# Fused attention and MLP backward: attention blocks in two passes, with a key quarter's exponentials turned by DMA

## The chip, the cores and the metric

The kernel runs on one core of a Trainium2 chip. The core has five engines with instruction streams of their own: PE (TensorE, matmuls), DVE (VectorE), ACT (ScalarE), POOL (GpSimd) and SP (SyncE, which here only issues DMAs). They run unsynchronized and wait for each other at semaphores. The metric is device time in microseconds of one execution, here the median of three runs: 2291.8 us (2291.62 to 2293.79). The profile is of one further execution.

## The reference

The program computes a forward pass and all gradients of it. With `xn = layernorm(x)`:

```python
def _A_ref(x, wqkv, wo):            # B, S, D = 1, 2048, 512; H = 32 heads, Dh = 16
    q, k, v = split_heads(x @ wqkv)
    scores = einsum("bhqd,bhkd->bhqk", q, k) * (Dh ** -0.5)
    p = softmax(scores)
    return merge_heads(einsum("bhqk,bhkd->bhqd", p, v)) @ wo

def _B_ref(x, w1, b1, w2, b2):      # F = 1792
    h = gelu(layernorm(x) @ w1 + b1)
    return h @ w2 + b2

out = x + _A_ref(xn, wqkv, wo) * silu(_B_ref(xn, w1, b1, w2, b2))
```

Outputs are `out` and the gradients of x, wqkv, wo, w1, b1, w2 and b2 for a given `grad_out`. In the backward pass of attention, with dO the gradient of a head's output, the gradient of the scores is dS = P * (dO V^T - rowsum(dO * O)). From it come dQ = dS K / 4 and dK = dS^T Q, and dV = P^T dO.

## The kernel before

There are three stages. `phase_pre` does the layernorms, projections and the MLP forward; attention starts near 157 us of the profile and ends near 1945; `phase3` does the remaining gradients. The change is in attention, with small parts of the other two.

`attention_core` handles the 32 heads in 16 pairs (p), the 2048 queries in four quarters (qc): 64 blocks (j). A block has 16 steps, one for each 128 keys (kb); a step index g counts through all blocks. All tiles hold two heads side by side, so a step's score tile is 128 keys x 2 x 512 queries.

In a step, `emit_s` (L1064) makes the scores with keys on the partitions, and ACT's exponential (L1092) writes them to `et`. Softmax sums aren't known yet, so `et` is not normalized; a shift taken off in the operands keeps it in range. `emit_d` (L1086) makes dO V^T for each head in a PSUM bank of its own, and DVE multiplies it with `et` into `gts` (L1103, two per step). `emit_a1` adds up over the steps, in the PSUM tile X, V and K weighted with `et` (L1126) and, through the constant `Lc`, the sums (L1123); `emit_a2` (L1136) adds the same for `gts`. After 16 steps X is copied out (L1141), transposed on PE in f32 (L1148), copied again (L1153), and `emit_finish` computes 1/sum, the row sums and, on POOL, the weights W1, W2, the outputs `Oall` and dQ in `dQall`.

For dK and dV the same matrices are needed with queries on the partitions. Each two steps' `gts` (128 x 2048 bf16) is turned by one DMA transpose issued by SP (L1112), into half of a map `gk` that holds one key quarter (kc). The exponentials are made a second time with queries on the partitions: `emit_t` (L1076) and ACT (L1097) into `e`. For one step in four of three key quarters they are turned instead, by eight PE transposes (L1048) and a DVE copy (L1053, `eE`). `emit_ze` (L1196) and `emit_zg` (L1204) add into the 64-row PSUM tile Z, with W1 and W2 as weights, and DVE adds Z into `acc` (L1219, L1221) or, in the last query quarter, into `ob` (L1223), which SP stores (L1225). This runs one block behind.

Once a pair, `load_pair` reads three operand tables (L1006 to L1008), POOL pads them into `KPad` and `QPad`, and SP turns these into KVT and QDT (L1019, L1022).

PE and DVE follow orders written out by hand for one block (`PE_ORDER`, `DVE_ORDER`), which a loop unrolls; ACT alternates the two kinds of exponentials. SP and POOL instructions are issued where the loop meets them. The MLP's last four token tiles and the last dO projections (`left_over`) are spread over the first 14 steps.

What matters of buffers: `et` 8 tiles of a step, `gts` 4 tiles of two steps, `gk` 6 maps, score tiles in PSUM 2, `d` one bank a head, and one bank shared in turn by Z, XT and ET.

Of the kernel before, what the change touches and what calls it, by code (L numbers as in the profile page):

```python
# [41 lines left out]
def phase_pre(ctx, tc, k, A_x, A_wqkv, A_wo, B_w1, B_b1, B_w2, B_b2, grad_out, opnds, psz, tailp):  # L42
# [138 lines left out]
    def kv_tile(g, i):  # L181
        proj(g, i, D, "pk", NS[g][:, :, i, :, 1:17])
        proj(g, i, 2 * D, "pv", NS[g][:, :, i, :, 17:33])
        proj(g, i, 0, "pq", NQ[:, :, 4 * g + i, :, 1:17])
        if i == 3:
            ts = slice(4 * g, 4 * g + 4)
            ns = NS[g]
            nc.sync.dma_start(out=k.NAT_s[g], in_=ns[:].rearrange("p a t j c -> p a t (j c)"))
            nc.gpsimd.tensor_copy(out=KPad[:, ts, 0:2, 0:17], in_=ns[:, 0, :, :, 0:17])
            nc.gpsimd.tensor_copy(out=KPad[:, ts, 2:4, 0:16], in_=ns[:, 0, :, :, 17:33])  # L190
            nc.gpsimd.tensor_copy(out=OP0["NAT"][:, ts], in_=ns[:, 0])
# [12 lines left out]
    def k_norm(g, i):  # L204
        norms(p1, kn2[:, 4 * g + i, :], NS[g][:, :, i, :, 1:17])

    with tc.manual_schedule(engines={ET_.PE, ET_.Activation, ET_.DVE, ET_.Pool, ET_.SP}):
# [4 lines left out]
        for g in range(4):  # L212
            NS[g] = p1.tile([128, NPAIR, 4, 2, NATW], bf16, name="NS", bufs=4)
            nc.gpsimd.memset(NS[g][:, :, :, :, 0:1], 1.0)
# [142 lines left out]
    def do_done(g):  # L357
        ts = slice(4 * g, 4 * g + 4)
        nd0 = ND[g][:, 0].rearrange("p t (j c) -> p t j c", j=2)
        nc.gpsimd.tensor_copy(out=QPad[:, ts, 2:4, 0:16], in_=nd0)  # L360
        if g >= 1:
            turn_q(g)
        nc.sync.dma_start(out=k.NATQd_s[g], in_=ND[g])
        nc.gpsimd.tensor_copy(out=OP0["NATQd"][:, ts], in_=nd0)

    def left_over(big, mid2, xt2, st2):


        w = [big.tile([128, 2, 16, 128], bf16, name="gk")[:].rearrange("p a b c -> p (a b c)") for _ in range(3)]

# [8 lines left out]
        load_do(3)  # L379
        v = {}  # L380

        def z(nm):
            return psz.tile([128, 512], f32, name=nm, tag="z")

        def first(t):
            m_mm(t, z("ps_m15"), 0, 7)

        def second(t):
            m_mm(t, None, 7, FC)
# [4 lines left out]
            th = xt2.tile([128, 4, 128], f32, name="xt")  # L394
            m_sig(mq[:, 0, :], th[:].rearrange("p a b -> p (a b)"), s[:, 0, :])
# [6 lines left out]
        def rest2(t):  # L402
            m_grad2(t, *v[t][0:3])

        def turn(_):
            pt = st2.tile([128, 4, IC, 128], bf16, name="dso_tp", tag="st")
            for i in range(4):
                for b in range(IC):
                    nc.tensor.transpose(pt[:, i, b, :], dso4[3][:, i, b * 128:(b + 1) * 128], k.ident_bf[:])
            nc.scalar.copy(out=dsoT[3], in_=pt[:])  # L410

        def do(t):

            g, i = divmod(t, 4)
            pd = st2.tile([128, 2, 512], f32, name="pd", tag="st")
# [3 lines left out]
            nc.scalar.copy(out=ND[g][:, :, i:i + 2, :].rearrange("p a n c -> p n a c"), in_=pd[:].rearrange("p n (a c) -> p n a c", a=NPAIR))  # L419
            if i == 2:  # L420
                do_done(g)
        steps = {g: [[], []] for g in range(14)}
        for n, t in enumerate(range(12, 16)):
            steps[2 * n][1].append((first, t))
            steps[2 * n + 1][1].append((second, t))
            steps[2 * n + 2][0].append((rest1, t))
            steps[2 * n + 3][0].append((rest2, t))
        for g, f in ((8, (do, 8)), (9, (do, 10)), (10, (turn, 0)), (11, (do, 12)), (12, (do, 14))):
            steps[g][1].append(f)
        def fill(_):  # L430
            w = z("fill")
            for n in range(2):
                nc.tensor.matmul(w[:], lhsT=woT[:, 0, 0:128], rhs=woT[:, 0, :], start=(n == 0), stop=(n == 1))
        steps[13][0].append((fill, 0))
        steps[13][1].append((fill, 0))
        return steps

# [16 lines left out]
    def row_shift3():  # L454
        for ts in (slice(0, 4), slice(4, 16)):
# [3 lines left out]
            if ts.start == 0:  # L459
                turn_q(0)  # L460
# [74 lines left out]
def phase3(ctx, tc, k, A_x, A_wqkv, A_wo, B_w1, B_w2, grad_out, out_0, out_1, out_2, out_3, out_4, out_5, out_6, out_7, dbg):  # L535
# [14 lines left out]
    with ExitStack() as c1:  # L550
# [13 lines left out]
        with ExitStack() as cL:  # L564
# [289 lines left out]
            dQT = dT.tile([128, NT, IC, 128], bf16, name="dQT", tag="dT")  # L854

            def turn_dq(q4):
                nc.sync.dma_start_transpose(out=dQT[:, q4 * 4:(q4 + 1) * 4].rearrange("p t c s -> p (t c) s"),
                                            in_=k.dQall[:, q4 * 4:(q4 + 1) * 4, :].rearrange("p t d -> p (t d)"))

            def load_r(h):  # L860
                nc.sync.dma_start(out=R[:, 4 * h:4 * h + 4], in_=k.dKVT_s.rearrange("(r p) s -> p r s", p=128)[:, 4 * h:4 * h + 4])
            later = [lambda: turn_dq(0), lambda: nc.sync.dma_start_transpose(out=wqT[:], in_=A_wqkv[:, 0:D]),
                     lambda: nc.sync.dma_start_transpose(out=wkvT[:], in_=k.WKVA_s), lambda: load_r(0), lambda: load_r(1),
                     lambda: turn_dq(1), lambda: turn_dq(2), lambda: turn_dq(3)]
# [15 lines left out]
        with ExitStack() as c2:  # L880
# [33 lines left out]
            for t in range(NT):  # L914
# [6 lines left out]
                for cc in range(IC):  # L921
                    nc.tensor.matmul(ps[:], lhsT=dQT[:, t, cc, :], rhs=wqT[:, cc, :], start=(cc == 0), stop=False)
# [27 lines left out]
PE_ORDER = """  # L950
a2:-1 zg:-7 d1:1 t:1 ze:-6 s:2 d0:1 zg:-6 ze:-5 zg:-5 t:2 d1:2 a1:0 s:3 d0:2 XT:-1 d1:3 s:4 a1:1 a1:2 t:4 d0:3 a2:0 ze:-4
a2:1 zg:-4 a2:2 ze:-3 s:5 d1:4 zg:-3 ze:-2 t:5 d0:4 zg:-2 ze:-1 zg:-1 s:6 d1:5 a1:3 a1:4 d0:5 t:6 E:3 s:7 a1:5 d0:6 s:8
d1:6 ze:0 a2:3 zg:0 ze:1 a2:4 t:8 d1:7 zg:1 s:9 d0:7 d1:8 ze:2 a2:5 d0:8 t:9 zg:2 s:10 d1:9 ze:3 a1:6 zg:3 t:10 d0:9 a1:7
a1:8 s:11 d1:10 E:7 s:12 d0:10 a1:9 d1:11 t:12 a1:10 a2:6 ze:4 a2:7 s:13 d0:11 zg:4 d1:12 a2:8 ze:5 d0:12 t:13 zg:5 a2:9
ze:6 a2:10 d1:13 s:14 d0:13 zg:6 a1:11 d1:14 t:14 a2:11 ze:7 zg:7 s:15 d0:14 a1:12 a2:12 d1:15 t:15 E:11 s:16 d0:15 a1:13
d1:16 t:16 a1:14 a2:13 ze:8 a2:14 zg:8 s:17 d0:16 a1:15 ze:9
"""
DVE_ORDER = """
m0:-5 m1:-4 m0:-4 m1:-3 m0:-3 m1:-2 acc:-9 m0:-2 m1:-1 eE:-5 m0:-1 m1:0 m0:0 xs:-1 m1:1 m0:1 acc:-5 m1:2 m0:2 xt:-1 m1:3
m0:3 sm:-1 m1:4 m0:4 acc:-1 m1:5 m0:5 eE:3 m1:6 m0:6 m1:7 m0:7 m1:8 m0:8 m1:9 acc:3 m0:9 m1:10 eE:7 m0:10 m1:11  # L960
"""


# [11 lines left out]
def attention_core(ctx, tc, opnds, ps_z, tail, NAT_s, NATQ_s, Oall, dQall, dKVT_out, ident_f32, ident_bf, npairs=16, nqc=4, turned=(0, 1, 2)):  # L975

    nc = tc.nc  # L980
    S = 2048
    ps_st = ctx.enter_context(tc.tile_pool(name="ps_st", reuse_waits="tile", bufs=2, space=PSUM))
    ps_d = ctx.enter_context(tc.tile_pool(name="ps_d", reuse_waits="tile", bufs=1, space=PSUM))
    ps_x = ctx.enter_context(tc.tile_pool(name="ps_x", reuse_waits="tile", bufs=1, space=PSUM))
    etp = ctx.enter_context(tc.tile_pool(name="etp", reuse_waits="tile", bufs=8))
    gtp = ctx.enter_context(tc.tile_pool(name="gtp", reuse_waits="tile", bufs=4))
    gbp = ctx.enter_context(tc.tile_pool(name="gbp", reuse_waits="tile", bufs=6))
    ep = ctx.enter_context(tc.tile_pool(name="ep", reuse_waits="tile", bufs=8))
    eep = ctx.enter_context(tc.tile_pool(name="eep", reuse_waits="tile", bufs=4))
    xsp = ctx.enter_context(tc.tile_pool(name="xsp", reuse_waits="tile", bufs=1))  # L990
    finp = ctx.enter_context(tc.tile_pool(name="finp", reuse_waits="tile", bufs=2))
    wp = ctx.enter_context(tc.tile_pool(name="wp", reuse_waits="tile", bufs=2))
    accp = ctx.enter_context(tc.tile_pool(name="accp", reuse_waits="tile", bufs=1))
    outp = ctx.enter_context(tc.tile_pool(name="outp", reuse_waits="tile", bufs=1))

    OP = opnds["OP"]
    KPad, QPad, Lc = opnds["KPad"], opnds["QPad"], opnds["Lc"]
    cur_op = {}
    load_q = []

    def load_pair(p):
        t = OP[p % 2]
        cur_op[p] = t

        def plain():
            nc.sync.dma_start(out=t["NAT"][:].rearrange("q (g k) j c -> q g (k j c)", g=4), in_=NAT_s[:, :, p].rearrange("g q k c -> q g (k c)"))  # L1006
            nc.sync.dma_start(out=t["NATQq"][:].rearrange("q k j c -> q (k j c)"), in_=NATQ_s[0][:, p])
            nc.sync.dma_start(out=t["NATQd"][:].rearrange("q (g k) j c -> q g (k j c)", g=4), in_=NATQ_s[1][:, :, p].rearrange("g q k c -> q g (k c)"))  # L1008

        def padk():  # L1010
            nc.gpsimd.tensor_copy(out=KPad[:, :, 0:2, 0:17], in_=t["NAT"][:, :, :, 0:17])
            nc.gpsimd.tensor_copy(out=KPad[:, :, 2:4, 0:16], in_=t["NAT"][:, :, :, 17:33])

        def padq():
            nc.gpsimd.tensor_copy(out=QPad[:, :, 0:2, 0:17], in_=t["NATQq"][:])
            nc.gpsimd.tensor_copy(out=QPad[:, :, 2:4, 0:16], in_=t["NATQd"][:])

        def turnk():
# [438 lines left out]
```

## Time and profile before

| | us |
|---|---|
| median of three runs | 2291.8 |
| the profiled execution, span | 2294.9 |
| attention, first to last transpose L1112 (start) | 169.0 to 1926.5 |
| transposes L1112 | 512, 4.5 from issue to landing (median) |
| PE busy | 2217.2 (97%) |
| DVE busy | 2041.7 (89%) |
| ACT busy | 2030.4 (88%) |
| POOL busy | 358.5 (16%) |
| granted TensorE clock, mean | 0.993 |

An engine's busy time is the time in which at least one of its instructions ran; instructions of one engine can overlap, so a busy engine may still have room, and the distance between two starts says more than a duration. In the profile L12 is line 12 of the kernel, PEld is the load of weights into PE, and "<-" ahead of a name means what ended a wait. SP's rows are the time in which it issued a DMA, not the time of the transfer. In the tables of stretches each engine has its busy time and a count, followed by the granted clock, the share of time that DMA packets were in flight, and GB/s.

### The profile page before, as it was taken

The page shows a single profiled execution, that of the slowest core. Times are in us where ns is not written, and L with a number is a line of the kernel's source. Part 1 is how long each engine was busy: PE and PEld are TensorE (multiplying, and loading weights), DVE is VectorE, ACT ScalarE, POOL GpSimd, SP SyncE. Part 2 cuts the span into 40 slices and gives each one's busy share as a digit, 9 for nine tenths or more (in the row PEclk, how much of TensorE's full clock was granted, in tenths as well). Part 3 has the DMA queues.
Part 4 walks back from the last instruction along what each step waited for, and adds up shares of the span by engine and source line. Part 5 has one row for each costly group of instructions (what it writes and reads, how often), then busy time and mean ns, then how long its engine had stood idle before and what let it go on. Part 6 is the DMA issues. An engine that isn't in the chain of part 4 may idle for free.

```text
span 2294.9 us, 50938 instructions
## 1 busy us (share of the span) xinstructions
PE 2217.2 (97%) x20089; PEld 794.7 (35%) x20135; DVE 2041.7 (89%) x3612; ACT 2030.4 (88%) x2322; POOL 358.5 (16%) x835
## 2 busy tenths in 40 slices
PE   7988999999999999999999999999999999879999
PEld 3433333333333333333333333333333333434544
DVE  7767999999999999999999999999999997789455
ACT  6767999999999999999999999999999998676243
POOL 4321111111111111111111111111111111421000
PEclk9999999999999999999999999999999999989999
DMA  9889999999999999999999999999999898987982
GB/s 290 276 268 181 167 179 164 185 162 183 162 183 164 179 163 180 166 179 170 175 175 166 180 165 184 160 183 165 181 165 179 157 162 208 226 187 151 126 241 70
DMA packets 1309744, 413.46 MB, mean 180 GB/s; under 512 B 1272416, under 2 KB 1286368, under 8 KB 1308864
## 3 DMA queue, kind: packets, MB, share of 16 engines
q1 hardware_dynamic: 1299056, 384.91, 90.5%
q0 software_dynamic: 6528, 20.06, 2.9%
q10 hardware_dynamic: 3920, 5.24, 0.7%
q8 instruction: 157, 2.57, 0.4%
q14 instruction: 83, 0.68, 0.1%
HBM read 44.42 MB, written 49.03 MB: 41 GB/s over the span
## 4 chain that ended last, share of the span: by engine, by line
PE 83%; DVE 8%; issue 4%; DMA 2%; ACT 2%; POOL 1%; SPq 0%; DVEq 0%; ACTq 0%; POOLq 0%
PE d L1086 12%; PE X L1123 12%; PE s L1064 11%; PE Z L1204 9%; PE X L1136 7%; PE Z L1196 5%; DVE gts L1103 5%; PE t L1076 5%; PE ET L1048 5%; PE ps_dw L789 2%; PE ps_dy L872 2%; PE ps_dhg L805 2%; PE XT L1148 2%; PE X L1126 1%; PE ps_dwkv L905 1%
## 5 line engine op out<-in xcount | busy, mean ns | idle before, releaser
L1103 DVE TENSOR_TENSOR gts<-d,et 128x512 bf16<-128x512 f32 x2048 | 1322.6, 685 | 70.2 <-issue 21.8
L1092 ACT ACTIVATE et<-s 128x1024 bf16<-128x1024 f32 x1024 | 1044.7, 1046 | 6.6 <-PE d L1086 6.4
L1097 ACT ACTIVATE e<-t 128x1024 bf16<-128x1024 f32 x832 | 867.6, 1044 | 23.1 <-PE t L1076 4.7
L1086 PE MATMUL d<-QDT,KVT 32*128 32x512 bf16 x2048 | 756.1, 383 | 19.9 <-DVE gts L1103 15.5
L1064 PE MATMUL s<-QDT,KVT 32*128 32x512 bf16 x2048 | 397.7, 384 | 2.5 <-ACT et L1092 2.0
L1204 PE MATMUL Z<-gk,W 128*32 128x512 bf16 x2048 | 396.9, 384 | 0.0
L1123 PE MATMUL X<-et,Lc 128*32 128x512 bf16 x2048 | 369.3, 388 | 0.0
L1126 PE MATMUL X<-et,NAT 128*32 128x512 bf16 x2048 | 368.3, 387 | 0.0
L1136 PE MATMUL X<-gts,NAT 128*17 128x512 bf16 x2048 | 330.4, 381 | 0.0
L1196 PE MATMUL Z<-e,W 128*32 128x512 bf16 x1664 | 321.5, 383 | 3.9 <-DVE ob L1223 1.2
L1076 PE MATMUL t<-KVT,QDT 32*128 32x512 bf16 x1664 | 323.2, 383 | 1.0 <-ACT e L1097 1.0
L1086 PEld LDWEIGHTS <-KVT 32*128 32x128 bf16 x2048 | 172.8, 91 | 232.1 <-issue 231.7
L1170 POOL TENSOR_TENSOR W<-NATQd,rL 128x128 bf16<-128x128 bf16 x64 | 25.7, 401 | 1124.2 <-DVE rL L1169 1124.2
L1064 PEld LDWEIGHTS <-KVT 32*128 32x128 bf16 x2048 | 105.7, 91 | 250.2 <-issue 230.6
L1204 PEld LDWEIGHTS <-W 128*32 128x32 bf16 x2048 | 100.2, 94 | 172.5 <-issue 142.0
L1076 PEld LDWEIGHTS <-QDT 32*128 32x128 bf16 x1664 | 92.3, 91 | 145.5 <-issue 140.6
L1196 PEld LDWEIGHTS <-W 128*32 128x32 bf16 x2048 | 105.2, 94 | 107.6 <-issue 97.0
L1123 PEld LDWEIGHTS <-Lc 128*32 128x32 bf16 x2048 | 83.4, 93 | 162.6 <-issue 162.5
L1053 DVE COPY eE<-ET 128x1024 bf16<-128x1024 bf16 x192 | 130.3, 678 | 4.4 <-PE ET L1048 4.4
L1048 PE MATMUL ET<-ident_bf,et 128*128 128x128 bf16 x1536 | 119.1, 220 | 2.1 <-DVE e L291 2.1
L1048 PEld LDWEIGHTS <-et 128*128 128x128 bf16 x1536 | 86.5, 98 | 45.5 <-issue 45.5
L1136 PEld LDWEIGHTS <-NAT 128*17 128x17 bf16 x2048 | 79.5, 89 | 59.7 <-issue 43.3
(215 smaller groups left out, 2357.3 us busy)
## 6 DMA issues: line engine op xcount, KB each, us to landing
gk<-gts SPq DMA_TRANSPOSE x512, 4.5
H1T_s<-h1p SPq DMA_DIRECT2D x28, 256.0 KB, 4.8
h<-H1T_s POOLq DMA_DIRECT2D x26, 256.0 KB, 4.1
HGT_s<-hgT SPq DMA_DIRECT2D x21, 256.0 KB, 4.5
NAT_s<-NS SPq DMA_DIRECT2D x4, 1056.0 KB, 5.3
gb<-GB_s SPq DMA_DIRECT2D x8, 512.0 KB, 5.4
Rkv<-dKVT_s SPq DMA_DIRECT2D x2, 2048.0 KB, 10.7
NAT<-NAT_s SPq DMA_DIRECT2D x15, 264.0 KB, 3.9
```

Of the source, the lines that this page charges most:

```text
L1048: nc.tensor.transpose(ET[:, hj, m * 128:(m + 1) * 128], st_et[g - 3 + m][:, hj, 384:512], ident_bf[:])
L1064: nc.tensor.matmul(s[:, hj, :], lhsT=op["KVT"][r, kb * 128:(kb + 1) * 128], rhs=op["QDT"][r, qc * 512:(qc + 1) * 512], start=True, stop=Tr ...
L1076: nc.tensor.matmul(t[:, hj, :], lhsT=op["QDT"][r, q0:q0 + 128], rhs=op["KVT"][r, kc * 512:(kc + 1) * 512], start=True, stop=True, tile_pos ...
L1086: nc.tensor.matmul(d[:], lhsT=op["KVT"][r, kb * 128:(kb + 1) * 128], rhs=op["QDT"][r, qc * 512:(qc + 1) * 512], start=True, stop=True, til ...
L1092: nc.scalar.activation(out=et[:], in_=st_s.pop(g)[:], func=ACT.Exp)
L1097: nc.scalar.activation(out=e[:], in_=st_t.pop(g)[:], func=ACT.Exp)
L1103: nc.vector.tensor_tensor(out=gts[:, g % 2, hj], in0=st_d.pop((g, hj))[:], in1=st_et[g][:, hj], op=ALU.mult)
L1123: nc.tensor.matmul(X[64 + 32 * hj:96 + 32 * hj, :], lhsT=Lc[:, :], rhs=et[:, hj, :], start=(kb == 0), stop=False, skip_group_check=True, t ...
L1126: nc.tensor.matmul(X[32 * hj:32 * hj + 32, :], lhsT=NATt[:, kb, hj, 1:33], rhs=et[:, hj, :], start=(kb == 0), stop=(kb == 15), tile_positi ...
L1136: nc.tensor.matmul(X[64 + 32 * hj:64 + 32 * hj + 17, :], lhsT=NATt[:, kb, hj, 0:17], rhs=gts[:, kb % 2, hj, :], start=False, stop=(kb == 1 ...
L1196: nc.tensor.matmul(Z[32 * hj:32 * hj + 32, :], lhsT=blk[j]["W1"][:, qb, hj, :], rhs=e[:, hj, :], start=(qb == 0), stop=False, tile_positio ...
L1204: nc.tensor.matmul(cur["Z"][32 * hj:32 * hj + 32, :], lhsT=blk[j]["W2"][:, qb, hj, :], rhs=grhs, start=False, stop=(qb == 3), tile_positio ...
```

## The change

A block now has two passes. The first makes scores, exponentials and sums alone: `a1` uses a table laid out as [V, 1, K] and yields O and the sums in rows 0 to 63 of X, without `Lc`. Then 1/sum, `W` = [dO/sum, dO O/sum] on POOL, its transpose on PE (DT) and a copy `dt`. In the second pass `d` multiplies a key operand [V, -1] with `dt`, so that `gts` = d * et is the finished dS. `a2` then adds dQ itself in rows 64 to 127 of X, scaled and copied by `emit_dq`, stored to DRAM and read back turned in `phase3`. Z has 128 rows: `ze` in 0 to 63, `zg` (weights `QW`, the plain queries) in 64 to 127.

For the last key quarter (`dmat=(3,)`) no `t` and no second exponential is made: SP turns `et` by DMA into a map, as it does `gts`. `E` and `eE` are gone. The second pass runs 21 steps behind the first (`lag`), Z 30 (`zlag`). `et` now has 12 tiles of two steps, four of them in the room of `dQall`; `gk` has 5 maps.

All five engines' orders come from `make_plan`, which advances a model of the engines with the durations in EST and picks at each point the operation that is due first under RULE. By the built order, SP issues 128 transposes of `et` (86 from `et`, 42 from `dQall`), PE has 33,092 rows for 40,012, ACT 768 second exponentials for 832.

```diff
-            nc.gpsimd.memset(NS[g][:, :, :, :, 0:1], 1.0)
+            nc.gpsimd.memset(NS[g][:, :, :, :, 16:17], 1.0)
...
+            for g in range(ts.start // 4, ts.stop // 4):
+                turn_q(g)
...
-            def turn_dq(q4):
-                nc.sync.dma_start_transpose(out=dQT[:, q4 * 4:(q4 + 1) * 4].rearrange("p t c s -> p (t c) s"),
-                                            in_=k.dQall[:, q4 * 4:(q4 + 1) * 4, :].rearrange("p t d -> p (t d)"))
+            def load_dq(h):
+                nc.sync.dma_start(out=dQT[:, 2 * h:2 * h + 2], in_=k.dQT_s.rearrange("(c p) s -> p c s", p=128)[:, 2 * h:2 * h + 2])
...
-                     lambda: turn_dq(1), lambda: turn_dq(2), lambda: turn_dq(3)]
+                     lambda: nc.sync.dma_start_transpose(out=k.dQall[:], in_=k.dQT_s)]
...
+NE, NET, NGT, NGK = 6, 12, 4, 5
+EST = dict(s=904, s_end=1040, pe=388, row=215, switch=315, act=100, pe_act=52, pe_dve=54, dve=60, wide=598, wide_end=681, half=330,
+           half_end=410, rl=200, pool=430, sp=2300, land=4800, sp_wait=120, map_wait=120)
+RULE = dict(per=1580, lag=21, tlag=24, zlag=30, zwait=2, tol=150, vtol=100, chain=-3, left=1.5)
+def sp_items(npairs, nqc, dmat):
+    out = []
+    for p in range(npairs):
+        for qc in range(nqc):
+            j = p * nqc + qc
+            o = [("g", (8 * j + n,)) for n in range(8)]
+            for kc in dmat:
+                o.insert(o.index(("g", (8 * j + max(2 * kc - 2, 0),))), ("e", (j, kc, 0)))
+                o.insert(o.index(("g", (8 * j + 2 * kc,))), ("e", (j, kc, 1)))
+            out += o
...
+    for p in range(npairs):
+        if p + 1 < npairs:
+            before(p, 8, ("ld", (p + 1,)))
+            before(p, 10, ("tk", (p + 1,)))
+            before(p, 18, ("tq", (p + 1,)))
+        if p:
+            before(p, 3, ("sq", (p - 1,)))
+            before(p, 6, ("sk", (p - 1,)))
...
+    def emit_a1(g):
+        j, kb = divmod(g, 16)
+        for hj in range(2):
+            nc.tensor.matmul(X[32 * hj:32 * hj + 32, :], lhsT=op_of(j)["NAT"][:, kb, hj, 0:32], rhs=et_of(g)[:, g % 2, hj],
+                             start=(kb == 0), stop=(kb == 15), skip_group_check=True, tile_position=(0, 32 * hj))
...
+    def emit_W(j):
...
+        nc.gpsimd.tensor_tensor(out=On[:], in0=xo, in1=rb, op=ALU.mult)
+        nc.gpsimd.tensor_tensor(out=W[:, :, :, 0:16], in0=OP[p % 2]["NATQd"][:, ts], in1=rb, op=ALU.mult)
+        nc.gpsimd.tensor_tensor(out=W[:, :, :, 16:32], in0=W[:, :, :, 0:16], in1=On[:], op=ALU.mult)
+        nc.gpsimd.tensor_copy(out=Oall[:, ts, p * 32:(p + 1) * 32].rearrange("q b (h c) -> q b h c", h=2), in_=On[:])
...
+    def emit_d(g, hj):
...
+        nc.tensor.matmul(d[:], lhsT=op_of(j)["KVT"][r, kb * 128:(kb + 1) * 128], rhs=tiles["dt", j][r, :],
+                         start=True, stop=True, tile_position=(64 + 32 * hj, 0))
...
+    def emit_map(k, src, j, kc, h):
+        nc.sync.dma_start_transpose(out=map_of(k, j, kc)[:, h], in_=src[:].rearrange("k a h q -> k (a h q)"))
+    def emit_dq(j):
...
+        nc.vector.tensor_scalar(out=cur["cq"][64:128, qc * 512:(qc + 1) * 512], in0=X[64:128, :], scalar1=0.25, scalar2=None, op0=ALU.mult)
...
+    def emit_sq(p):
+        cq = tiles.pop(("cq", p))
+        for hj in range(2):
+            nc.sync.dma_start(out=dQT_out[p * 32 + hj * 16:p * 32 + hj * 16 + 16, :], in_=cq[64 + 32 * hj + 16:64 + 32 * hj + 32, :])
...
+    def emit_sk(p):
+        ob = tiles.pop(("ob", p))
+        for hj in range(2):
+            for x in range(2):
+                r0 = p * 64 + hj * 32 + 16 * x
+                nc.sync.dma_start(out=dKVT_out[r0:r0 + 16, :], in_=ob[64 * x + 32 * hj:64 * x + 32 * hj + 16, :])
...
+    with tc.manual_schedule(engines={ET_.PE, ET_.Activation, ET_.DVE, ET_.Pool, ET_.SP}):
+        for t in QW:
+            nc.gpsimd.memset(t[:, :, :, 16:32], 0.0)
+        emit_qw(0)
+        f.update(tail(gbp, ep, accp, ps_st))
+        for _, kind, i in make_plan(npairs, nqc, dmat):
+            f[kind](i)
```

In the order SP's item `g` is a transpose of `gts`, `e` of `et`; `ld` are the three loads of the next pair, `tk` and `tq` its operand transposes; `sq` and `sk` store dQ and dK, dV. The left-over work of the MLP is now part of the plan and stands, with the first 18 steps of scores, ahead of the first `d`.

## The prediction

> **What bounds the kernel now.** I read the page first, then the busy time by stretches, then the groups, then SyncE's (SP's) own timeline. One pair of heads is four blocks; the transposes of the score matrix to the out-projection at the end of one pair (L1148, first 214.5 us, last 1929.5, 64 of them) are 63 periods apart, so a block takes 1715.0 / 63 = 27.2 us and a pair 108.9. Steady pair (busy us and count of PE, PEld, DVE, ACT, POOL, then granted clock, DMA share, GB/s):
>
> ```profile
> span 2294.9 us, 50938 instructions
> 323.30:432.00 108.70, 107.78 (x1114) 35.61 (x1112) 104.37 (x177) 107.56 (x117) 14.46 (x40) 1.00 0.99 176
> ```
>
> Three engines are full at once: PE 99%, ACT 99%, DVE 96%. ACT runs 29 exponentials a block: 108.7 / 116 = 0.937 us apart, though one lasts 1.04 (they overlap). The groups of the page that set this:
>
> ```profile
> L1103 DVE TENSOR_TENSOR gts<-d,et 128x512 bf16<-128x512 f32 x2048 | 1322.6, 685 | 70.2 <-issue 21.8
> L1092 ACT ACTIVATE et<-s 128x1024 bf16<-128x1024 f32 x1024 | 1044.7, 1046 | 6.6 <-PE d L1086 6.4
> L1097 ACT ACTIVATE e<-t 128x1024 bf16<-128x1024 f32 x832 | 867.6, 1044 | 23.1 <-PE t L1076 4.7
> ...
> L1053 DVE COPY eE<-ET 128x1024 bf16<-128x1024 bf16 x192 | 130.3, 678 | 4.4 <-PE ET L1048 4.4
> L1048 PE MATMUL ET<-ident_bf,et 128*128 128x128 bf16 x1536 | 119.1, 220 | 2.1 <-DVE e L291 2.1
> ```
>
> The fourth resource is the queue of DMA transposes on SP. "DMA share 0.99" does not show that it is full, since packets that wait are counted; SP's timeline does (start, length, instruction, count):
>
> ```profile
> 222.99 25.45 SPq L1112 DMA_TRANSPOSE gk<-gts  x9
> 325.16 8.60 SPq L1112 DMA_TRANSPOSE gk<-gts  x3
> 333.86 0.56 SPq L1225 DMA_DIRECT2D dKVT_s<-ob  x1
> 334.50 21.93 SPq L1112 DMA_TRANSPOSE gk<-gts  x8
> ...
> 1080.59 3.54 SPq L1019 DMA_TRANSPOSE KVT<-KPad  x1
> 1084.22 3.17 SPq L1022 DMA_TRANSPOSE QDT<-QPad  x1
> 1087.49 7.32 SPq L1112 DMA_TRANSPOSE gk<-gts  x3
> 1094.90 0.63 SPq L1225 DMA_DIRECT2D dKVT_s<-ob  x1
> 1095.62 22.65 SPq L1112 DMA_TRANSPOSE gk<-gts  x8
> ```
>
> After the two operand transposes of a pair (L1019, L1022) each row starts where the last ended: the queue is behind and shows its own pace. Per transpose: (25.45 + 8.60 + 21.93 + 7.32 + 22.65) / 31 = **2.77 us**, from 7.32 / 3 = 2.44 to 8.60 / 3 = 2.87. Now 34 are wanted in a pair (32 L1112 and two operands), 34 x 2.77 = 94 of 108.9 us, and the queue needs some ten transposes to catch up by 108.9 / 32 - 2.77 = 0.63 us each. The data rate agrees. Same columns as above:
>
> ```profile
> 1083.00:1117.00 34.00, 33.77 (x352) 11.18 (x349) 32.68 (x58) 33.72 (x38) 3.31 (x10) 1.00 1.15 194
> 1043.40:1045.40 2.00, 2.00 (x26) 0.64 (x21) 1.96 (x4) 2.00 (x3) 0.00 (x0) 1.00 1.09 210
> 1048.40:1049.40 1.00, 1.00 (x12) 0.31 (x15) 1.00 (x3) 0.86 (x2) 0.00 (x0) 1.00 1.27 290
> GB/s 216 214 168 167 10 155 290 266 218 192 214 217 198 219 218 208 207 148 45 98 291 240 208 249 112 214 213 204 213 208 205 201 0 34 286 291 289 191 219 210
> ```
>
> A transpose moves 128 x 2048 x 2 = 524,288 bytes: 2.70 us at 194 GB/s over a backlog of 34 us. The last row is that backlog in 40 slices of 0.85 us: about 210, a standstill (10, 45, 0), then 290 until the lost time is made good. At 210 (a lone transpose) it would be 2.50 us, at 290 1.81.
>
> **The change part by part.**
>
> *ACT*: 64 exponentials go (832 to 768): 28 for 29 a block, 64 x 0.937 = -60 us if ACT sets the pace, down to a pair of 105.1.
>
> *DVE*: 192 eE copies go (-130.3 us), and dl and ndr (64 x (0.205 + 0.299) = -32.3). New: one scaled copy dq and one copy dt a block, each 64 partitions of 512, priced at L1221 (64x512, 679 ns): +87; bounds 0.2 (the 128x8 reciprocal) and 0.69. xt halves: 0 to -0.48 each, I take -0.3, so -19. Sum -95 us, 5.9 a pair; DVE falls to 98.5 of 108.7 and is not on the path.
>
> *PE*: 2048 matmuls with Lc (beside those with NAT, on other columns, so worth nothing to twice 0.21 us a step), 1536 E transposes (119.1) and 128 t go; 256 small DT transposes come (the order has them; at 220 ns or less, 56 us at most). PE gets room either way. Scores s now run 21 steps ahead of d, in the built order.
>
> *POOL* falls from some eleven operations a block to four. But their chain xs, XT, xt, rL, three POOL operations, DT, dt now stands in front of the next block's d: 0.68 + 0.66 + 0.4 + 0.2 + 3 x 0.40 + 0.4 + 0.6 = 4.1 us. The order puts seven d (three and a half steps, 6 us at 27.2 / 16 = 1.7) between the last a1 of a block and the first d that needs dt; they hide it, and four gts buffers, some 11 us of transposes, hide a stumble. Without that cover 1 us a block would be 64 us.
>
> *SP queue*: 128 transposes of et (86 from et, 42 from dQall, all 128x16x128 as L1112's), 8 a pair: **+22 us**. The dKVT_s store becomes four of 64 KB, and two dQT_s stores come. A pair is then 42 transposes and 9 plain DMAs. At L1225's median issue of 0.55 us for eight and L1006's 0.94 for one, the plain ones are 5.3 us. 42 x 2.77 + 5.3 = **121.6 us a pair**, against 108.9 now and ACT's 105.1. So the queue overtakes ACT. Waits in this queue: a transpose of et stands some seventeen steps behind its exponential, so it never waits. The KPad turn (L1019 now) stands two transposes (5.5 us) behind the load of its pair, which needs 3.9 us to land (L1006's median) and two POOL copies (0.69 + 0.62): 5.2, just covered; uncovered 1 us a pair, 16 in all, with the next gts behind it. Maps fall from six buffers to five, with five filled a block: one of gts is held for about two transposes, a landing of 5 and 2 of Z work, 12.5 us, that of et for six transposes, some 24: 4 x 12.5 + 24 = 74 of 5 x 30.4 = 152 us of buffer, so none waits.
>
> What is late then: gts is freed at landing, so the products wait, so d, then s by the ring of et; zg waits for its map. The order leaves d five steps past the map that a zg waits for, so that two transposes or more stand behind the awaited one and the queue isn't drained. For its pace I choose 2.77, not 2.50 or 1.81, because no stretch of more than three transposes holds the others. Bounds: 2.44 and 2.92 (9.21 + 22.94 us for 11 at 1631.29).
>
> [...]
>
> *Start*: the left-over gate work used to run beside d from 157.5 us; now all of it, and 18 s, stand before the first d. 18 exponentials (16.9 us), four gates (1.33 each) and the copies make about 28 us of ACT, so the first transpose goes at about 190, not 169: **+21**, bounds +10 and +40.
>
> *End*: four dQT transposes become two plain loads and one transpose of 2 MB from DRAM. L919's two of that size took 24.17, so about 12 us on SP; SP waits 21.4 us there before L884 (for ps_dy), which hides it: 0, at most +12. The four query transposes at the start move to one place: 0 to +5, within the start's bounds.
>
> *Sum*, in the profiled time: 190 + 16 x 121.6 - 7.5 (the last pair loads and turns no successor) = 2128 for the queue's last transpose, now at 1926.5 + 2 = 1928.5. So +200: 2294.9 + 200 = 2495. The median of the runs, 2291.8, is 3 below this profile: **2490**. At 2.70 us each the sum is 2440, at 2.87 2560: this case's own range is 2430 to 2570.
>
> **The rivals.**
>
> *ACT decides (faster).* If transposes in a row run at 290 GB/s, the queue needs 42 x 1.81 + 5.3 = 81 us and a pair follows ACT's 105.1: -60, up to -120 if the new order packs the exponentials to 0.90 (closest spacing seen, a start at 999.83 and the next at 1000.73 in the timeline); with +10 to +20 at the start 2190 to 2250. For it: 290 is reached for 3 us at a time. Against: only after a standstill. [...] Chance 0.12.
>
> *The queue at a lone transpose's pace.* At 2.47 us a pair is 109.0, no change, plus start: 2260 to 2330. For it: 7.32 / 3. Against: the standstills in the 34 us row. 0.08.
>
> *Queue and in-order PE lock (slower still).* PE stands at a zg whose map is late, d behind it is not issued, and the queue runs dry before the next product. If that costs 0.4 us at each of 256 maps, +100 on top: 2570 to 2700. For it: transposes land 4.5 us after issue, longer under backlog. Against: the two or three waiting gts. 0.14.
>
> The forecast itself has 0.66.
>
> **How the numbers follow.** 2250 to 2600 leaves out the ACT rival (0.11) and half of the lock (0.07). What a measurement can tell from no change is about 0.2% (5 us). Faster: 0.12 and 0.035 of the lone pace; same 0.02; slower the rest.
>
> **What would show it.** In the changed profile: SP's timeline without gaps, rows of transposes at 2.7 to 2.9 us each; a block at 30.4 us; exponentials 30.4 / 28 = 1.09 us apart, so that they no longer overlap (ACT still shows 28 x 1.044 / 30.4 = 96%, which is not its limit); DVE or PE waiting for "DMA gk". Wrong if the transposes are closer than 2.5 us, if exponentials come under 0.98 us apart, or if SP waits for products while blocks are longer than 28 us.

## The result, and the profile after

The changed kernel takes 2511.6 us (median of four runs, 2504.6 to 2521.6), the old one beside it 2291.7 (four runs): 1.0964 times as long, 95% interval 1.0935 to 1.0993. In the experiments below, ratios leave out runs that took over 1.5% longer than the fastest of the same kernel (two of four in e3, one of four in e9). Forecast were 2490 us, 2430 to 2570 for that case alone. Direction, size and the named resource came out, the size in part by luck. But the profile shows a second thing that no step of the forecast has. First the clock row of the old kernel's page (granted TensorE clock in 40 slices, tenths) and its matmul group d:

```profile
PEclk9999999999999999999999999999999999989999
L1086 PE MATMUL d<-QDT,KVT 32*128 32x512 bf16 x2048 | 756.1, 383 | 19.9 <-DVE gts L1103 15.5
```

The same of the changed kernel, with its span and the groups that answer to those shown of before:

```profile
span 2508.5 us, 44491 instructions
PEclk9999787878787677878897888777788788799999
L1493 DVE TENSOR_TENSOR gts<-d,et 128x512 bf16<-128x512 f32 x1376 | 899.9, 684 | 192.1 <-PE d L1489 92.7
L1432 ACT ACTIVATE e<-t 128x1024 bf16<-128x1024 f32 x768 | 811.4, 1058 | 120.6 <-PE t L1424 64.2
L1489 PE MATMUL d<-dt,KVT 32*128 32x512 bf16 x2048 | 845.3, 452 | 26.0 <-DVE gts L1493 17.6
L1428 ACT ACTIVATE et<-s 128x1024 bf16<-128x1024 f32 x688 | 713.6, 1059 | 75.2 <-PE d L1489 25.8
```

A product on DVE lasts 684 ns as before, an exponential some 13 ns more, but a d matmul 452 ns for 383, and the clock is 0.6 to 0.8 in all but one slice of attention (mean over the span 0.836, before 0.993). DVE and ACT now wait mostly for PE. The clock's records hold only 1.0 and 0.5: 826 us at half clock, before 34. Two blocks of one pair, and the pair (busy us and count of PE, PEld, DVE, ACT, POOL, then clock, DMA share, GB/s):

```profile
316.70:342.90 26.20, 25.35 (x227) 7.91 (x225) 24.74 (x42) 26.02 (x29) 1.42 (x4) 1.00 1.14 198
406.30:439.30 33.00, 32.35 (x227) 7.40 (x225) 25.40 (x42) 27.46 (x29) 1.42 (x4) 0.64 0.97 167
316.70:439.30 122.60, 116.93 (x899) 30.46 (x897) 100.64 (x165) 107.56 (x113) 8.06 (x20) 0.78 1.09 188
```

The same 227 matmuls take 26.2 us at full clock and 33.0 at 0.64. At full clock ACT is busy 26.02 of 26.20 and the block is shorter than the old 27.2; at half clock PE is busy 32.35 of 33.0 and is the limit. SP's timeline in that pair (start, length, instruction, count):

```profile
334.74 1.32 SPq L1509 DMA_DIRECT2D dQT_s<-cq  x2
336.15 3.00 SPq L1496 DMA_TRANSPOSE gk<-gts  x1
339.26 2.27 SPq L1496 DMA_TRANSPOSE gk<-et  x1
341.62 5.75 SPq L1496 DMA_TRANSPOSE gk<-gts  x2
347.45 1.81 SPq L1496 DMA_TRANSPOSE gk<-et  x1
349.31 2.55 SPq L1553 DMA_DIRECT2D dKVT_s<-ob  x4
351.96 5.15 SPq L1496 DMA_TRANSPOSE gk<-gts  x2
```

Each row starts about 0.1 us after the last one ended: a full queue, as forecast. Over 215 to 1850 us a transpose takes 2.51 us of SP on the mean, and SP stands still for 152 of 1635 us, 98 of them in gaps of over 0.2 us. SP is done with the issue of a transpose of gts 5.4 us (median) after its product on DVE ended, before 2.6: the queue is a transpose or more behind. But 60 of the long gaps, 94 us together, end 0.03 us after the product that the next transpose needs, and 77 of these us lie at half clock. So the queue is now and then short of work, mostly where PE is slow. By the first transpose of X in each block, 63 blocks last 30.19 us on the mean, before 27.22: 187 of the profile's 213.6 us. The rest is at the start and the end.

### The profile page after: what moved, and what is told of

It is laid out like the page before. It is cut to its first block, busy times and chain, and to the rows that moved or that the text cites. A ratio compares the mean times of both kernels' runs of the same rounds, so it can differ in the third digit from the quotient of the medians.

```text
span 2508.5 us, 44491 instructions
## 1 busy us (share of the span) xinstructions
PE 2342.4 (93%) x16631; PEld 717.2 (29%) x16675; DVE 1975.2 (79%) x3420; ACT 2016.9 (80%) x2258; POOL 257.6 (10%) x512
## 5 line engine op out<-in xcount | busy, mean ns | idle before, releaser
L1493 DVE TENSOR_TENSOR gts<-d,et 128x512 bf16<-128x512 f32 x1376 | 899.9, 684 | 192.1 <-PE d L1489 92.7
L1489 PE MATMUL d<-dt,KVT 32*128 32x512 bf16 x2048 | 845.3, 452 | 26.0 <-DVE gts L1493 17.6
L1428 ACT ACTIVATE et<-s 128x1024 bf16<-128x1024 f32 x688 | 713.6, 1059 | 75.2 <-PE d L1489 25.8
L1493 DVE TENSOR_TENSOR gts<-d,dQall 128x512 bf16<-128x512 f32 x672 | 440.7, 684 | 105.3 <-PE d L1489 51.0
L1528 PE MATMUL Z<-gk,QW 128*32 128x512 bf16 x2048 | 479.8, 470 | 7.5 <-DMA gk<-gts 7.4
L1443 PE MATMUL X<-gts,NAT 128*32 128x512 bf16 x2048 | 476.5, 462 | 1.1 <-DVE gts L1493 0.6
L1428 ACT ACTIVATE dQall<-s 128x1024 bf16<-128x1024 f32 x336 | 347.5, 1057 | 41.3 <-PE d L1489 18.4
L1437 PEld LDWEIGHTS <-NAT 128*32 128x32 bf16 x2048 | 102.4, 96 | 383.6 <-issue 383.5
L1437 PE MATMUL X<-dQall,NAT 128*32 128x512 bf16 x672 | 156.2, 461 | 0.0
L1520 PE MATMUL Z<-gk,W 128*32 128x512 bf16 x512 | 125.4, 489 | 1.3 <-DVE ob L1544 0.8
L1443 PEld LDWEIGHTS <-NAT 128*32 128x32 bf16 x2048 | 102.8, 96 | 34.2 <-issue 33.8
L1528 PEld LDWEIGHTS <-QW 128*32 128x32 bf16 x2048 | 104.2, 99 | 13.6 <-DMA gk<-gts 8.4
```

The lines of the kernel that those rows point to most:

```text
L1428: nc.scalar.activation(out=et_of(g)[:, g % 2], in_=tiles.pop(("s", g))[:], func=ACT.Exp)
L1437: nc.tensor.matmul(X[32 * hj:32 * hj + 32, :], lhsT=op_of(j)["NAT"][:, kb, hj, 0:32], rhs=et_of(g)[:, g % 2, hj], start=(kb == 0), stop=(k ...
L1443: nc.tensor.matmul(X[64 + 32 * hj:96 + 32 * hj, :], lhsT=op_of(j)["NAT"][:, kb, hj, 1:33], rhs=gts_of(g // 2)[:, g % 2, hj], start=(kb == ...
L1489: nc.tensor.matmul(d[:], lhsT=op_of(j)["KVT"][r, kb * 128:(kb + 1) * 128], rhs=tiles["dt", j][r, :], start=True, stop=True, tile_position= ...
L1493: nc.vector.tensor_tensor(out=gts_of(g // 2)[:, g % 2, hj], in0=tiles.pop(("d", g, hj))[:], in1=et_of(g)[:, g % 2, hj], op=ALU.mult)
L1520: nc.tensor.matmul(cur["Z"][32 * hj:32 * hj + 32, :], lhsT=tiles["W", j][:, qb, hj, :], rhs=rhs_of(tiles["e", j, kc], hj, qb) if e is None ...
```

## The experiments

Theories, as they stood at first: the queue of transposes sets the pace and the clock falls because PE waits (queue theory); or PE at half clock is a cause of its own (PE, later clock theory). The first four runs:

**e1, without turned et.** The 128 transposes of et are left out, and the last key quarter's Z reads the map of gts in their place (its dV is not computed).

```diff
-             rhs=rhs_of(tiles["e", j, kc], hj, qb) if e is None else ...
+             rhs=rhs_of(tiles["g", j, kc], hj, qb) if e is None else ...
...
-             e=lambda i: emit_map("e", et_of(...), *i),
+             e=lambda i: None,
```

> The changed kernel without its 128 transposes of et: the last key quarter's Z takes the map of gts in place of that of et, so dV of that quarter is not computed; every other instruction and every order stays. Queue theory (42 transposes a pair at 2.77 us and 5.3 us of plain DMAs set the pace): 34 x 2.77 + 5.3 = 99.5 us a pair falls below ACT's 105.1, so a pair takes 105 to 109 and the whole 2240 to 2310 us, with the granted clock of attention back above 0.95. Rival, PE sets the pace (its granted clock is 0.80 in attention and its order is new): its work is unchanged, so 2450 us or more and a clock near 0.80.

Measured: 2407.7 us, 1.0487 (1.0418 to 1.0556), clock 0.888. Between the two: without the turned et 104 of the 220 us go, and 116 stay. The blocks show why. Two that follow each other, in the windows of this run:

```profile
283.50:309.60 26.10, 25.18 (x227) 7.86 (x225) 24.59 (x42) 25.91 (x29) 1.42 (x4) 1.00 0.96 169
309.60:341.60 32.00, 31.27 (x227) 7.39 (x225) 25.28 (x42) 27.17 (x29) 1.42 (x4) 0.68 0.74 142
```

The work is the same, and the queue is not full (169 and 142 GB/s); one block has half clock for 20 us and is 5.9 us longer. PE's timeline at the point where it drops (some lines left out):

```profile
307.44 0.39 PE L1424 MATMUL t<-KVT,QDT 32*128 32x512 bf16 x2
307.62 0.37 PE L1489 MATMUL d<-dt,KVT 32*128 32x512 bf16 x1
308.34 0.39 PE L1414 MATMUL s<-QDT,KVT 32*128 32x512 bf16 x2 [0.34 <-ACT et L1428]
...
309.58 0.46 PE L1454 MATMUL XT<-ident_f,xs 64*128 64x64 f32 x4
310.17 0.39 PE L1414 MATMUL s<-QDT,KVT 32*128 32x512 bf16 x2
...
310.83 0.38 PE L1489 MATMUL d<-dt,KVT 32*128 32x512 bf16 x1
311.14 0.61 PE L1520 MATMUL Z<-e,W 128*32 128x512 bf16 x2
311.15 0.61 PE L1528 MATMUL Z<-gk,QW 128*32 128x512 bf16 x2
311.69 0.61 PE L1414 MATMUL s<-QDT,KVT 32*128 32x512 bf16 x2
```

Around the small transposes of X there are few matmuls, and from 311.1 us each lasts 0.61 us for 0.38. All 28 drops of this run lie 1.1 to 1.6 us after the first of these transposes. PE was hardly idle: in the 3.41 us ahead of each of the 28 it stood still for 0.5 us at most, never over 0.35 at a time.

**e2, twice the turned et.** Each transpose of et is issued a second time, into a spare tile.

```diff
+    def emit_more(i):
+        emit_map("e", src, *i)
+        nc.sync.dma_start_transpose(out=spare[i[2]][:], in_=src[:].rearrange("k a h q -> k (a h q)"))
```

> The changed kernel with each of the 128 transposes of et issued a second time, into a spare tile that nothing reads. Queue theory: 50 transposes a pair, 8 x 2.77 = 22.2 us more, 16 x 22.2 = +355, so 2830 to 2880 us; at the 2.56 us that a late transpose takes here, +328. Rival, PE or its order sets the pace and the queue still has the 171 of 1934 us in which SP issues nothing: most of that is used first, so less than +200, under 2710 us.

Measured: 2810.9 us, 1.2233 (1.2194 to 1.2271), clock 0.771. 299 us for 128 more, 2.34 each: far more than the rival's 200, a little less than the 328 to 355 of the queue theory. SP's time splits into 50 transposes a pair at this run's 2.53 us, 5.3 of plain DMAs and 8.1 of gaps, 140 us; that is an account of measured parts and no test of its own. The clock fell further (PE is busy for 87% of attention), but SP stands still for only 95 of 1635 us: the queue sets the pace here.

**e3, each d twice.**

```diff
-        nc.tensor.matmul(d[:], lhsT=op_of(j)["KVT"]..., rhs=tiles["dt", j][r, :], ...)
+        for _ in range(2):
+            nc.tensor.matmul(d[:], lhsT=op_of(j)["KVT"]..., rhs=tiles["dt", j][r, :], ...)
```

> The changed kernel with each of the 2048 d matmuls done twice into the same bank: more PE work, nothing else. It tells whether PE is what is short. Queue theory: PE has room, so 2490 to 2540 us whatever the granted clock does. Clock theory (PE is granted 0.80 because it idles, and that slows the loop): the clock rises towards 0.95 and the time falls by 100 us or more. PE-bound theory: 2048 x 0.215 us more on PE, +300 us or more at the lower clock, 2800 us.

Measured: 3111.5 and 3127.3 us, 1.3596 (1.3543 to 1.3648), clock 0.711; more than any theory gave. The page of this run:

```profile
PEclk9977556556959597556595975568587555569999
L1490 PE MATMUL d<-dt,KVT 32*128 32x512 bf16 x4096 | 1490.8, 515 | 14.3 <-DVE gts L1494 13.4
```

Slices at 9 and at 5: 21 blocks at full clock last 30.1 us, 29 with over 40 us of half clock 45.9. At full clock 32 more matmuls cost 4 us a block (30.1 for 26.1), 0.12 each; the 0.30 each over the whole run is mostly clock. So half clock has a price of its own. And more matmuls do not bring the clock back by themselves (mean 0.711 here, 0.836 without them): the second d goes to the same rows, columns and bank as the first, behind it and not beside it (0.12 us each, where the zero matmuls of e6 below cost 0.04).

**e4, all on ACT.** `dmat=()`: no et is turned, and ACT makes the second exponentials of the last key quarter too, 32 exponentials a block for 28.

```diff
-... npairs=16, nqc=4, dmat=(3,)):
+... npairs=16, nqc=4, dmat=()):
```

> The changed kernel with dmat=(): all second exponentials on ACT, no transposes of et, two passes and the list scheduler as they are. Queue theory: 34 transposes a pair are 99.5 us, ACT's 32 exponentials a block at 0.937 us are 119.9 us a pair, so ACT sets the pace: 2440 to 2490 us, ACT 97% busy. Rival, the two passes or the new order are what costs: at least 2510 us, since PE gets 256 t matmuls more and loses nothing.

Measured: 2545.3 us, 1.1092 (1.1064 to 1.112), clock 0.916. A miss: the time lies in the rival's range. A pair lasts 123.0 us (median), almost without spread: 0.961 us for each of 128 exponentials, some 3 us a pair more than expected. SP's queue has room here (521 of 1635 us in gaps), ACT is busy for 96% of attention, and 58 of 61 blocks have up to 8 us of half clock. This looks like ACT's bound with the clock in it. This run alone does not exclude that the new order costs something; e1 speaks against it, since its blocks at full clock take 26.15 us, 0.934 for each of 28 exponentials.

The next four runs were to separate queue and clock. The old kernel has 10.2 matmuls per us in attention, the changed one 8.2 in its stretches at full clock and 6.2 in those at half clock. In e5 and e6 two matmuls with a table of zeros stand beside each a1, on the 64 columns of X that it leaves free, where the old kernel had Lc (in its trace 1796 of 2048 matmuls with Lc start within 0.02 us of one with NAT); they add nothing to the result (1984 of them in all, 992 pairs).

**e5, zero matmuls beside a1; e6, the same without turned et.**

```diff
+        if g >= 32:
+            for hj in range(2):
+                nc.tensor.matmul(X[64 + 32 * hj:96 + 32 * hj, :], lhsT=zero[:], rhs=et_of(g)[:, g % 2, hj],
+                                 start=False, stop=False, skip_group_check=True, tile_position=(0, 64 + 32 * hj))
```

> The changed kernel with 1984 x 1 more pairs of matmuls: beside a1 of every step from step 32 on, two matmuls with a table of zeros on the other 64 columns, which add nothing to X[64:128] (they stand where the old kernel had Lc). Nothing else changes. Clock theory (the granted clock follows the rate of matmuls: 10.2 per us at a clock of 1.00 before, 8.2 to 8.5 per us in the stretches at full clock and 5.5 to 6.2 in those at half clock after; half clock is a cause of lost time, not only a sign of waits): the mean clock rises to 0.95 or more and the time falls by the share that the run without turned et left over, to 2370 to 2430 us. Queue theory (the transposes alone set the pace, the clock falls because PE waits): clock up a little, time 2490 to 2530. Rival that any more PE work costs time, as the doubled d did (0.31 us for each matmul): 2700 or more.

> The zero matmuls beside a1 and no turned et (Z's V part of the last key quarter reads the map of gts, so dV of that quarter is not computed). Both suspected causes are gone. If queue and clock are the two causes and add up: clock 0.95 or more and 2240 to 2310 us, the 105 us a pair that ACT's 28 exponentials a block allow. If the 115 us that were left without the turned et belong to the new order or its waits and not to the clock: 2380 to 2430, as without the zero matmuls (2408). If more PE work costs time: above 2430.

Measured: e5 2480.4 us, 1.0807 (1.0784 to 1.083), clock 0.941; e6 2360.8 us, 1.0296 (1.0278 to 1.0315), clock 0.973. A pair of each (windows; first e5):

```profile
316.00:435.00 119.00, 112.93 (x1035) 31.76 (x1031) 100.86 (x168) 107.50 (x114) 8.10 (x20) 0.94 1.12 195
```

```profile
311.90:421.90 110.00, 105.83 (x1026) 30.88 (x1024) 99.30 (x165) 106.01 (x113) 8.10 (x20) 1.00 0.99 172
```

More matmuls, and less time: from the third block to the last the half clock falls from 744 to 188 us (e5), and without turned et from 451 to 31 (e6), where 28 drops become 3. So matmuls beside others bring the clock back, and half clock is a cause of lost time. But with the clock mended the time of the whole kernel falls by 31 us only; none of e5's three ranges was met, and the queue theory's 2490 was nearest. In e5 SP stands still for 84 of 1635 us, 25 of them in gaps of over 0.2: the queue is full nearly all the time, and a pair is 42 x 2.57 + 5.3 + 6 = 119 us. Without the queue's load (e6) it is 110, or 27.5 us a block, where e1 has 26.1 at full clock: the 32 zero matmuls of a block cost 1.4 us (0.04 each), 88 us in 63 blocks. Without them e6 would come to 2273 us (an estimate from these two numbers); with them it met neither of its two ranges.

All blocks of four runs from the third on, sorted by the time that the clock's records have at half clock in them (blocks: mean us), counted from the traces (e1's is of its fastest run, 2387.0 us):

```
half-clock time in the block   under 0.5 us   0.5 to 8    8 to 16    over 16
changed kernel                 14: 26.2       7: 29.0     17: 31.3   23: 32.5
e1, no turned et               33: 26.2       10: 28.4    -          18: 32.2
e5, zero matmuls               33: 28.0       20: 31.1    8: 33.0    -
e6, both                       58: 27.5       -           3: 31.2    -
```

A block costs the same by its clock, turned et or not: 26.2 or 32. What the turned et add is more drops: they start 1 to 2 us into a block in e1, in the changed kernel also 9 to 14 and 17 to 25 us into it.

**e7, the old kernel without Lc.** Lc is left out in 15 of 16 steps.

```diff
-        for hj in range(2):
+        for hj in range(2 if kb == 0 else 0):
             nc.tensor.matmul(X[64 + 32 * hj:96 + 32 * hj, :], lhsT=Lc[:, :], ...
```

> The kernel before with the two Lc matmuls of 15 of 16 steps left out (the softmax sums are then those of one step alone; the outputs of attention are not the reference's). These matmuls run beside those with NAT on other columns. Clock theory: with 8.4 to 9 matmuls per us for 10.2 the clock falls below 0.97 in places and the time rises by 0.5% or more (2305 to 2400 us), although the kernel has less to do. Rival (the clock has another cause, such as waits of PE): clock 0.99 and 2285 to 2295.

Measured: 2284.1 us, 0.9951 (0.9934 to 0.9968), clock 0.989. A miss for the clock theory as worded: 9.2 matmuls per us, and no drop from 260 us to the end of attention. The rival's 2285 to 2295 is met within 1 us. PE is busy for 99% of attention here, as in the kernel before. Leaving out Lc is not enough by itself.

**e8, the pace alone.** Sixty transposes ahead of everything else in the old kernel.

```diff
+        for n in range(60):
+            tdst = tp.tile([128, 16, 128], bf16, name="tdst", bufs=8)
+            nc.sync.dma_start_transpose(out=tdst[:], in_=tsrc[:].rearrange("k a h q -> k (a h q)"))
```

> The kernel before with 60 transposes of a 128x2048 bf16 tile, issued by SP one after the other into eight tiles ahead of everything else: no engine computes beside them. If a transpose's pace is its own (194 GB/s in the backlogs), they stand 2.45 to 2.75 us apart here too, and the row adds 150 to 165 us. If what runs beside them (code fetches, other reads of SBUF) slows them in attention, they stand at 1.8 to 2.3 us, 105 to 140 us in all.

One run: 2440.7 us, 147 more than before. SP's timeline, and the shortest, median and longest of the 60 (ns):

```profile
3.42 157.56 SPq L1381 DMA_TRANSPOSE tdst<-tsrc  x60
L1381 SPq DMA_TRANSPOSE tdst<-tsrc x60: 1893/2458/6745, 3.4 to 154.2; - x60
```

and 40 us of it in the windows:

```profile
60.00:100.00 40.00, 0.00 (x0) 0.00 (x0) 0.00 (x0) 0.00 (x0) 0.00 (x0) 0.50 1.12 211
```

The first and the last take over 6 us, so 157.56 / 60 = 2.63 is too high for the pace. From the fifth start to the last it is 2.48 us each with nothing beside them, as 524,288 bytes at 211 GB/s give. That is the first expectation's pace, though the row adds 147 us and not its 150 to 165. So most of the pace belongs to the transposes, not to what attention does beside them; that they take 2.51 to 2.63 in the full queues there is a small rise whose cause stays open. 42 of them at 2.48 are 104.2 us, with the plain DMAs 109.5: the old pair's 108.9 is used up, and nothing is left for gaps.

The last four runs tried to mend both.

**e9 and e10, zero matmuls in the last four steps of a block; e9 without turned et.**

```diff
-        if g >= 32:
+        if g >= 32 and kb >= 12:
```

> As the run without turned et (2408 us), with zero matmuls beside a1 only in the last four steps of a block (8 a block for 32). There all 28 drops of the clock came 1.1 to 1.6 us after the transposes of X began, that is after the lull in which PE waits for the copy of X (4.4 and 6.7 matmuls in the two us before, 6.8 to 13 in those around), and a block lasted 26.1 us at full clock, about 32 with a drop. If this lull is what the gate answers to, the drops go, blocks stay at 26.1 to 26.4 us, clock 0.97 or more: 63 x 26.3 + 612 around them = 2260 to 2300 us. If the mean rate decides (8.6 per us at full clock there, 9.2 with 32 zero matmuls), most drops stay: 2360 to 2410.

> The changed kernel with zero matmuls in the last four steps of a block alone, nothing left out. Queue and clock theory together: the drops at a block's turn go (26 of 52), those behind a late map stay; clock 0.88 to 0.95; a pair follows the queue at 42 x 2.55 + 9 x 0.55 plain + about 5 of short gaps = 118 to 119.5 us: 15.75 x 119 + 612 = 2470 to 2495. If the clock were the larger part of the loss: 2400 or less. If the lull doesn't matter: 2505 to 2520.

Measured: e9 2371.6 to 2395.1 us, 1.0451 (1.0409 to 1.0494), clock 0.905; e10 2520.2 us, 1.0967 (1.0917 to 1.1016), clock 0.861. Both miss the theory that the lull alone decides, and both lie where the other side was expected: e9 within the 2360 to 2410 of the mean rate, e10 at the edge of the 2505 to 2520 of a lull that doesn't matter. Both intervals overlap those without the zeros (e1, the changed kernel), so a gain isn't shown. The drops became 19 for 28 and 42 for 52. The lull moved rather than filled: in the second us ahead of the transposes of X there are now 8.9 matmuls for 3.8, in the last one 3.0 for 6.8 (means over the blocks of e9 and e1). Filling in one place was too little.

**e11, plain DMAs off SP; e12, et turned in three of four query quarters.** Both on top of e10.

```diff
-        nc.sync.dma_start(out=t["NAT"]...          (three loads, six stores of a pair)
+        nc.gpsimd.dma_start(out=t["NAT"]...
...
-            for kc in dmat:
+            for kc in (dmat if qc < 3 else ()):
```

> As the one before, with the nine plain DMAs of a pair (three operand loads, two stores of dQ, four of dK and dV) issued by POOL, so that SP's queue holds transposes alone. Queue theory (SP's issue is serial: what stands in it adds up): 42 x 2.55 + about 5 of gaps = 112 us a pair, 2360 to 2410 us. If the DMA engines' total rate decides and not SP's queue: within 1% of the run before, 2460 to 2500. If POOL's issue holds up the weights of the next block: above 2500.

> As the one before, with the last key quarter's et turned in three of four query quarters only; in the fourth block of a pair ACT makes the exponentials again (116 a pair as in the old kernel, for 112). Queue 40 x 2.55 + about 4 = 106 us, ACT 116 x 0.933 = 108.2: the pair follows ACT at 108 to 110, 15.75 x 109 + 612 = 2310 to 2350 us. If the queue still sets the pace some other way (maps, landings): 2360 or more. If the old kernel's pair with the new orders and full clock is enough to win: below 2290.

Measured: e11 2499.1 us, 1.0892 (1.0845 to 1.094); its interval overlaps e10's, so a gain isn't shown. The transposes took 2.63 us each for 2.53: what SP no longer issued between them came back in their own length. That fits the second expectation (within 1% of e10): not SP's instruction count adds up but the transfers. e12 2555.9 us, 1.1141 (1.1102 to 1.1179), a miss by 200 us. SP stands still for 329 of 1635 us, so the queue does not bind. Two blocks that follow each other:

```profile
502.30:534.10 31.80, 31.09 (x279) 9.17 (x277) 29.72 (x50) 31.26 (x35) 1.42 (x4) 1.00 1.14 194
534.10:565.40 31.30, 27.50 (x192) 6.97 (x192) 20.90 (x34) 23.55 (x25) 1.42 (x4) 0.73 0.78 144
```

One block has ACT full at full clock (35 of its instructions in 31.3 us), the next has only 192 matmuls and loses its clock. The planner, whose lags were kept, spreads the exponentials unevenly; whether a tuned order would mend it was not tried. No version of the changed kernel beat the old one.

## Why the prediction was right in size, and where it was wrong

*Which resource.* Right in the main. Without the turned et 104 us go; with the clock mended 120 (e5 to e6); twice the turned et cost 299. With the clock mostly mended (e5) the kernel is still 186 us slower than before.

*The queue's term, 42 x 2.77 + 5.3 = 121.6 us a pair.* A pair took 120.8 us (4 x 30.19), but only because two errors cancel, which is luck. SP's time in it is 104.4 us of transposes (2.51 each), 5.1 of plain DMAs and 11.3 of standing still, which the forecast put at nothing: 5.7 of them are waits for products at half clock, some 4 the 0.1 us between issues. The step that failed here is the choice of 2.77 "because no stretch of more than three transposes holds the others": the backlog of before held standstills (10, 45 and 0 GB/s in the row shown), and the pace with nothing beside it is 2.48. That is the pace of the rival that had 0.08. With 2.51 the forecast's own sum would have given 2317 us, within that rival's 2260 to 2330; what lifts the time from there is SP's standing still and the later start. In e5, where the clock is mended, less standing still (6 us) is made up by slower transposes (2.57). The last gts transpose, forecast for 2128 us, starts at 2137.9. (What the prediction calls transposes of the score matrix, L1148, are those of X, one set at the end of each block; its 27.2 us hold.)

*"PE gets room either way".* This step failed outright. Fewer matmuls gave PE a lower clock (16631 instructions for 20089, mean clock 0.836 for 0.993), not room. With over 16 us of half clock a block takes 32 us whatever the queue does (32.5, and 32.2 without the turned et), and that is most of what stayed without the turned et. The two losses overlap: mending the clock alone gives 31 us (2511.6 to 2480.4), because the queue needs 119 a pair anyway; without the queue's load it would give about 134, an estimate (63 x (28.27 - 26.15), the mean block of e1 against its full-clock block). With zero matmuls, which cost time themselves, it gave 47 (e1 to e6).

*ACT -60.* Right where ACT sets the pace: 26.15 for 27.22 us in blocks at full clock, 67 us over 63 blocks, seen in e1 and in 14 blocks of the changed kernel. The rival "ACT decides" names what the kernel would be with neither loss.

*Start +21, end 0.* The first transpose went at 208.9, not 190: +40, the upper bound. ACT waits between the left-over gates (8.0 us in one place at 172 us), where 28 us of unbroken work were assumed. From the last gts transpose to the end it is 370.6 us, before 368.4: the end's 0 holds.

*Signs.* Exponentials 1.08 us apart (1.09 forecast), the block at 30.2 (30.4), SP's rows end to end: seen. Rows of transposes at 2.7 to 2.9 us each: not seen, 2.51 (just above the 2.5 that would have spoken against). DVE or PE waiting for "DMA gk": hardly, DVE 12.1 us in all and the Z matmuls that read a map 7.4; ACT, not named, 31.9. DVE waits for PE. The lock rival needs 0.4 us at each of 256 maps, 102 us of waits at the maps; 7.4 rule it out. A sign against, SP waiting for products while blocks are over 28 us, is there in part: 98 of 1635 us.

*What the clock answers to.* The changes of the clock lie on a grid of 3.413 us. In the traces of before and after all 132 of them lie on it, within 0.002 us. In e1 it is not a long stretch of idle time that goes ahead of a drop: the 28 drops come after at most 0.35 us of idle at a time, and PE is busy for 93% of the changed kernel's span. Counted from all fourteen traces on that grid, from the first to the last transposes of X: windows of 3.41 us by the matmuls that start in them, and by PE's busy share as the profile has it (with modelled ends).

```
windows at full clock          all     followed by half clock
matmuls  up to 19              228     174
         20 to 23              332     120
         24 and 25             470      82
         26 and more          4752      24
PE busy  under 80%             247     196
         80 to 90%             381     141
         90 to 95%            1098      62
         95% and more         4056       1

windows at half clock          all     followed by full clock
matmuls  up to 19              837      15
         20 to 25             1005     295
         26 and more           119      93
PE busy  95% and more         1763     401
         of these in e3        494      19
```

The clock is lost after windows in which PE was short of work, by either measure, and the two go together. e7 is better told by the busy share: 25 windows under 26 matmuls and no drop, 23 of them over 90% busy. But the way back is not told by it: at half clock PE is full nearly all the time (1763 of 1961 windows at 95% and more) and stays there, in e3 for 41 to 181 us at a stretch, and the windows that lead back are those with many matmuls (93 of 119 with 26 and more, 15 of 837 with up to 19). That fits e5 and e6, where the added matmuls run beside others (0.04 us of a block each), and e3, where they don't (0.12). Which quantity the clock answers to stays open; whether rows, columns or kinds of matmul weigh differently wasn't tried.

## What to carry to other kernels

Work that lies beside other work on PE may be what holds its clock (in e6 32 zero matmuls a block took half clock from 451 to 31 us): before taking it out for nothing, count the matmuls that stay per window of 3.4 us (the grid of the clock's changes here), above all at the turns of a loop (all 28 drops of e1). A row of the same transfers at the start of a kernel gives a queue's pace with nothing beside it; take it from start to start, without the first and the last. It is a lower bound (2.48 us here, 2.51 to 2.63 beside attention), so ask whether the sum leaves room for products that come late. Two losses that cover each other give back little when one is mended alone, so test them together too.

## What the runs showed of the hardware that was not expected

PE fell to half clock while its page row shows 93% busy; the row alone does not tell it, the matmul's mean (452 for 383 ns) and the clock row do. Thirty-two matmuls of zeros a block cost 1.4 us at full clock, and a block that kept its clock by them took 27.5 us for some 32. At half clock PE could be full and stay at half: in e3 19 of 494 such windows were followed by full clock. Transposes of 128x2048 bf16 within SBUF ran at 211 GB/s, 2.48 us each, with nothing beside them; a pair of the changed kernel moves 188 in all.
